# Spacing the weight decodes of a linear-attention and two-MLP kernel: one empty part more in the first group, a pace of 2.5 and three empty parts in the two whole-product MLP pairs

## The chip, the cores and the metric

The kernel runs on one core of a Trainium2 chip. The metric is the device time of one execution in microseconds (us). The engines are TensorE (PE in the profile, PEld for its weight loads), VectorE (DVE), ScalarE (ACT), GpSimd (POOL) and SyncE (SP), which issues the transfers. Each engine works through its own instructions in the order in which the program wrote them and waits on semaphores for the others.

## What is computed

Linear attention over 4 x 8 heads, then two MLPs, on 2304 tokens of 512 features, in float32. The two MLPs are the part that the change touches:

```python
def _moe_ref(x, w_gate, w_val, w_out, rms_g):      # d_ff 1536: "kind 1" in the kernel
    rms = np.sqrt(np.mean(x * x, axis=-1, keepdims=True) + 1e-06)
    xn = x / rms * rms_g
    g = xn @ w_gate
    silu = g * (1.0 / (1.0 + np.exp(-g)))
    val = xn @ w_val
    return (silu * val @ w_out).astype(np.float32)

def _moe2_ref(x, w_in, w_out):                     # d_ff 2048: "kind 2"
    h = x @ w_in
    g = h * (1.0 / (1.0 + np.exp(-h)))
    return (g @ w_out).astype(np.float32)
```

The weights arrive as 64-bit floats. The kernel reads the two 32-bit words of each number and makes of them a float32 in integer arithmetic (this is what a decode does), and it then splits every float32 operand into a high half, rounded to TensorE's format, and a low half, the rest. A product is three matmuls: high x high, high x low, low x high (`PASS`).

## The kernel before

**Data.** The tokens lie in five blocks j = 0 to 4 (512 tokens each, block 4 has 256). `xs[j]` holds the inputs of the current MLP as high and low halves, `ya[j]` the sums of its outputs. The hidden features are taken in slices f of 128.

**Groups.** After the attention part the slices run in 17 groups, u = 0 to 16. Groups 0 to 8 are GLU slices f = 3 to 11 (kind 1; slices 0 to 2 come before them, in the attention part and at the start of the loop `stream`). Groups 9 to 16 are MLP pairs (kind 2, two slices f each). Most groups multiply blocks 0 and 1 in `quad`, with seven half products instead of eight: for that, sums of the weights (`sum12`, `sum34`, `shi`, `slo`) and sums of the tokens (`token_sums`: `whole` on VectorE L345, `less` on GpSimd L319, `tok_high` on ScalarE L328, `tok_low` on VectorE L331) are made. The first two MLP pairs, u = 9 and 10 (`std <= u < std + NSTD`), take the whole products of blocks 0 and 1 instead, in `mlp_block`; the tokens' sums of the new `xs` are made beside them. These are the whole-product pairs, pair 1 and pair 2 below.

**What a block's product sets off.** In a GLU slice: matmuls for g (L205), Silu on ScalarE (L222), matmuls for v, s = s * v on VectorE (L228), and `split_h`, that is the high half of h on ScalarE (L198) and the low half on VectorE (L199). In an MLP slice: matmuls (L205), Silu (L239, or L661 in `mlp_block`), and `split_h`. Later come the output products of a block, four of them (`g2_glu`, L259, or `g2_mlp`, L292), which read both halves of h, and whose results are added to `ya` by VectorE (L270 in the GLU, L303 in the MLP; in pair 1 ScalarE copies them, L301). The outputs go through a ring of four PSUM buffers named y. In the last GLU slice L270 is followed by the halves of the next MLP's inputs (L272 on ScalarE, L249 on VectorE).

**The weight queue.** `WeightQueue` holds a list of jobs, here called parts. Each part is a count of free weight slots that it needs and some functions, and a part `(0,)` has none and is empty. The functions are:

- `dec(key, n)`: five VectorE steps on the words of a weight (L146, L149, L152, L154, L157) and two GpSimd integer adds (L160). The weight lies in the buffers raw0, m0 or raw1, m1.
- `load(u, key, n)`: a DMA of 512 KB on SP's queue into raw0 or raw1, for the next weight that uses that buffer. It stands in the same part behind the `dec` that frees the buffer.
- `hi(key)`: ScalarE writes the high half (L412); for g and v it first scales the rows (L168, four steps).
- `lo(key)`: VectorE writes the low half (L416); then the weight can be used.
- `shi`, `slo`: the same for the sums of the weights, L412 and L416.

Here a0 and a1 are the two weights that a group's first products use (g and v, or the two `i`), and bs those of its output products (o, or the two `p`).

**What sets the order.** The program writes TensorE's work by the generator `stream`. Each `yield` hands out the time of some matmuls (matmuls x columns / 2365 us). The loop at the end adds it to `due`; when `due` is over the pace it issues the next part (`tick`) and takes the pace off. The pace is `A_PACE` 1.8 up to u = 8 and `M_PACE` 2.0 after that. While `hold` is set no part goes; `need` issues parts at once until a weight is ready. In `g1_glu` and `proj` the yield comes ahead of the matmuls, and in `g2_glu` and `g2_mlp` behind them. So a part's instructions stand in each engine's order at the place where the sum passed the pace: a decode in front of L228 is done before L228. The tokens' sums come out one by one the same way, by `gone`.

In pair 1, `each` says how many output products of the last GLU slice follow each half of an `mlp_block`: the pairs of numbers are for the first and second half. The jobs of pair 1 itself are issued in groups 7 and 8; a job that needs 1 << 10 slots ends them and holds the queue until pair 1's products of blocks 0 and 1 are out. Then the jobs of pair 2 go, beside pair 1's other blocks, and the jobs of group 11 behind them.

Of the kernel before, what the change touches and what calls it, by code (L numbers as in the profile page):

```python
# [20 lines left out]
def kernel(  # L21
# [168 lines left out]

    PASS = [(0, 0), (0, 1), (1, 0)]
    HALVES = [slice(0, 64), slice(64, P)]
    M_PACE, A_PACE, T_PACE = 2.0, 1.8, 1.2
    W_EARLY, GRAIN, GATE = 3, 3, 3

    def split_h(s, j):
# [114 lines left out]
    NSTD = 2  # L311
    std = next(u for u, g in enumerate(groups) if g[0] == 2)
# [55 lines left out]
    class WeightQueue:  # L368
# [28 lines left out]
        def plan(self, u):  # L397
            kind, _ = groups[u]
            (a0, a1), bs = self.keys(u)
            st = self.st  # L400
            ss = State()
            ss.t = {}
            hw = KH * P
            mf = lambda key: st[key].m.bitcast(F32)

            def dec(key, n):
                for k in range(7):
                    w_decode((0, 0, key, None), st[key], k, n)

            def split_hi(x, tl):  # L410
                v = tl.rearrange("p (a n) -> p a n", a=2)
                nc.scalar.activation(out=v[:, 0, :], in_=x, func=AF.Copy)  # L412
                return v

            def split_lo(x, v, eng=nc.vector):
                eng.tensor_tensor(out=v[:, 1, :], in0=x, in1=v[:, 0, :].bitcast(F32), op=ALU.subtract)  # L416

            def hi(key):
                if key[1] in "gv":
                    w_scale(st[key])  # L420
                st[key].t = split_hi(mf(key), self.slot(key))

            def lo(key):
                split_lo(mf(key), st[key].t)
                wt[key] = st[key].t

            def sum12():
                ss.x = pools["w"][1].tile([P, KC * P], F32, tag="ws", name="ws", bufs=1)
                m0, m1 = mf(a0), mf(a1)
                less(ss.x[:, :hw], m1[:, :hw], m1[:, hw:], ALU.add)  # L430
                less(ss.x[:, hw:], ss.x[:, :hw], m0[:, :hw])

            def sum34():
                m0, m1 = mf(a0), mf(a1)
                less(m1[:, :hw], m0[:, :hw], m1[:, :hw])
                less(m1[:, hw:], m0[:, hw:], ss.x[:, hw:])

            def shi(n):
                ss.t[n] = split_hi(ss.x if n == 0 else mf(a1), self.slot(("s", u, n)))

            def slo(n):
                split_lo(ss.x if n == 0 else mf(a1), ss.t[n], nc.vector if kind == 2 else nc.gpsimd)
                wt["s", u, n] = ss.t[n]

            load = self.load
            if u == 0:
                jobs = [
                    (0, lambda: dec(a0, 0), lambda: load(u, bs[0], 0)),
                    (0,),
                    (0, lambda: dec(a1, 1), lambda: load(u + 1, 1, 1)),  # L450
                    (1, lambda: hi(a0)),
                    (0, lambda: lo(a0)),
                    (1, lambda: hi(a1)),
                    (0, lambda: lo(a1), sum12),
                    (0, sum34),
                    (1, lambda: shi(0)),
                    (0, lambda: slo(0), lambda: dec(bs[0], 0), lambda: load(u + 1, 0, 0)),
                    (1, lambda: shi(1)),
                    (0, lambda: slo(1)),
                ]  # L460
                self.tail = [(1, lambda: hi(bs[0])), (0, lambda: lo(bs[0]))]
            elif kind == 1:
                jobs = [
                    (0, lambda: dec(a1, 1), lambda: load(u + 1, 1, 1)),
                    *self.tail,
                    (0, lambda: dec(a0, 0), lambda: load(u, bs[0], 0)),
                    (1, lambda: hi(a1)),
                    (0, lambda: lo(a1)),
                    (1, lambda: hi(a0)),
                    (0, lambda: lo(a0), sum12),  # L470
                    (0, sum34),
                    (1, lambda: shi(0)),
                    (0, lambda: slo(0), lambda: dec(bs[0], 0), lambda: load(u + 1, 0, 0)),
                    (1, lambda: shi(1)),
                    (0, lambda: slo(1)),
                ]
                self.tail = [(1, lambda: hi(bs[0])), (0, lambda: lo(bs[0]))]
            elif std <= u < std + NSTD:
                jobs = [
                    (0, lambda: dec(a1, 1), lambda: load(u, bs[1], 1)),  # L480
                    *self.tail,
                    (0, lambda: dec(a0, 0), lambda: load(u, bs[0], 0)),
                    (1, lambda: hi(a1)),
                    (0, lambda: lo(a1)),
                    (0, lambda: dec(bs[1], 1), lambda: load(u + 1, 1, 1)),
                    (1, lambda: hi(a0)),
                    (0, lambda: lo(a0)),
                    (0, lambda: dec(bs[0], 0), lambda: load(u + 1, 0, 0)),
                    (1, lambda: hi(bs[1])),
                    (0, lambda: lo(bs[1])),  # L490
                    (0,),
                    (1, lambda: hi(bs[0])),
                    (0, lambda: lo(bs[0])),
                ]
                self.tail = []
                if u == std:
                    jobs.append((1 << 10,))
            else:
                jobs = [
                    (0, lambda: dec(a0, 0)),  # L500
                    (0, lambda: dec(a1, 1), lambda: load(u, bs[0], 0)),
                    (1, lambda: hi(a0), lambda: load(u, bs[1], 1)),
                    (1, lambda: lo(a0), lambda: hi(a1)),
                    (0, lambda: lo(a1), sum12),
                    (0, sum34),
                    (1, lambda: shi(0)),
                    (0, lambda: slo(0)),
                    (1, lambda: shi(1), lambda: dec(bs[0], 0)),
                    (0, lambda: slo(1), lambda: load(u + 1, 0, 0)),
                    (1, lambda: hi(bs[0]), lambda: dec(bs[1], 1)),  # L510
                    (0, lambda: lo(bs[0]), lambda: load(u + 1, 1, 1)),
                    (1, lambda: hi(bs[1])),
                    (0, lambda: lo(bs[1])),
                ]
            self.jobs += [(n, fns) for n, *fns in jobs]
# [13 lines left out]
    wq = WeightQueue()  # L529
# [144 lines left out]
    def stream():  # L674
# [25 lines left out]
        for u, (kind, fs) in enumerate(groups):  # L700
            first, last = kind == 2 and fs[0] == 0, u == len(groups) - 1
            done = u + 1 == std
            wq.pace = A_PACE if u < std else M_PACE
            hs = {j: {} for j in range(NB)}
            if std <= u < std + NSTD:
                out_of = lambda j: g2_mlp(fs, j, hs[j], first, False, False)
# [1 line left out]
                wq.hold = first  # L708
                while wait:
                    wait.pop(0)()  # L710
                each = [(2, 1)] * 4 if first else [(2, 2), (1, 1), (0, 0), (0, 0)]
                for n, k in enumerate(each):
                    if n == 3:
                        ys = chain_of(ys, out_of(0))
# [856 lines left out]
```

## Time and profile before

| | |
|---|---|
| median of 3 runs | 963.65 us (962.95 to 964.86) |
| the profiled execution | 964.62 us |
| its span, first to last instruction | 962.7 us |
| mean granted clock of TensorE | 0.994 |
| TensorE / weight loads | 947.6 / 793.8 us busy |
| VectorE | 709.2 us busy |
| ScalarE | 432.8 us busy |
| GpSimd | 415.3 us busy |
| DMA | 60.42 MB, mean 63 GB/s |

The rows below are from the profiled execution, in us from the start of its span. A timeline row gives the start, the time from there to the end of the last instruction of the row, the engine, the line and the operation with what it writes and reads, and how many; in brackets stands how long the engine was idle before and who released it. The end of a matmul is modelled; matmuls overlap, so their pace is read from the starts. The attention part takes the first 180 us, the GLU slices run to about 565 us, pair 1 to about 612 us, pair 2 to about 664 us, and the other six MLP pairs to the end.

### The profile page before, as it was taken

What the parts mean: (1) busy time and instruction counts of PE and PEld (TensorE: products, weight loads), DVE (VectorE), ACT (ScalarE), POOL (GpSimd) and SP (SyncE); (2) the same over time, 40 slices, a digit from 0 to 9 for tenths busy, and PEclk for the clock granted to TensorE, in tenths of its full rate; (3) what the DMA queues carried; (4) which work ended last, traced back from release to release, by engine and by line L of the source; (5) the groups of instructions that cost most, each with busy time, mean ns of one, the idle gap of its engine ahead of it and who ended that gap; (6) DMA issues with size and microseconds to landing.
All of it is one profiled execution on the core that took longest, in us unless ns stands there. A gap on an engine that the chain in (4) does not pass through costs nothing.

```text
span 962.7 us, 17025 instructions
## 1 busy us (share of the span) xinstructions
PE 947.6 (98%) x6570; PEld 793.8 (82%) x6570; DVE 709.2 (74%) x1368; ACT 432.8 (45%) x978; POOL 415.3 (43%) x402
## 2 busy tenths in 40 slices
PE   8999999998999999999999999999999999999998
PEld 6888878887888888888888886788888888888887
DVE  6998989656687778788779785886666666767653
ACT  6999877543334424333333345433333333333321
POOL 8888645315455336436335204632424242424200
PEclk9999999999999999999999999999999999999999
DMA  8655543002120121022012101111111111111023
GB/s 188 174 134 136 138 122 101 9 23 66 44 78 32 44 66 45 22 65 66 22 45 66 44 1 44 45 44 44 44 45 45 44 44 44 44 44 45 1 77 121
DMA packets 79489, 60.42 MB, mean 63 GB/s; under 512 B 27312, under 2 KB 73648, under 8 KB 79408
## 3 DMA queue, kind: packets, MB, share of 16 engines
q1 hardware_dynamic: 79136, 59.26, 21.1%
q8 instruction: 52, 0.85, 0.4%
q14 instruction: 29, 0.24, 0.1%
q10 hardware_dynamic: 272, 0.07, 0.0%
HBM read 49.87 MB, written 4.72 MB: 57 GB/s over the span
## 4 chain that ended last, share of the span: by engine, by line
PE 90%; DVE 4%; ACT 2%; DMA 1%; POOL 1%; SPq 1%; issue 1%; DVEq 0%; POOLq 0%
PE g L205 22%; PE y L292 20%; PE g L535 15%; PE y L259 13%; PE y L205 6%; PE b L1039 3%; PE b L205 2%; PE b L1439 2%; PE kv L1119 2%; PE b L1012 2%; PE b L1223 2%; PE b L1199 1%; PE b L1319 1%; POOL m L160 1%; DVE h L199 1%
## 5 line engine op out<-in xcount | busy, mean ns | idle before, releaser
L160 POOL TENSOR_TENSOR m<-m,raw 128x512 int32<-128x512 int32 x136 | 204.1, 1503 | 323.7 <-issue 176.9
L205 PE MATMUL g<-xs,w 128*128 128x512 f32 x1056 | 256.3, 389 | 0.0
L205 PEld LDWEIGHTS g<-xs,w 128*128 128x128 f32 x1056 | 197.4, 188 | 40.5
L292 PE MATMUL y<-w,h 128*128 128x512 f32 (+1 forms) x870 | 209.4, 390 | 4.2 <-DVE h L199 3.3
L292 PEld LDWEIGHTS y<-w,h 128*128 128x128 f32 x870 | 163.1, 189 | 40.0 <-DVE h L199 4.7
L259 PE MATMUL y<-h,w 128*128 128x512 f32 (+1 forms) x648 | 157.4, 369 | 2.7 <-ACT h L198 2.5
L199 DVE TENSOR_TENSOR h<-s,h 128x512 fp32r<-128x512 f32 (+1 forms) x134 | 108.4, 815 | 65.5 <-ACT h L198 64.2
L270 DVE TENSOR_TENSOR ya<-y,ya 128x512 f32<-128x512 f32 (+1 forms) x200 | 123.0, 631 | 22.5 <-PE y L259 22.4
L259 PEld LDWEIGHTS y<-h,w 128*128 128x128 f32 x648 | 114.4, 190 | 24.0 <-ACT h L198 2.9
L303 DVE TENSOR_TENSOR ya<-y,ya 128x512 f32<-128x512 f32 (+1 forms) x127 | 84.6, 680 | 60.2 <-PE y L292 59.6
L198 ACT ACTIVATE h<-s 128x512 fp32r<-128x512 f32 (+1 forms) x134 | 77.2, 586 | 100.3 <-DVE s L640 46.2
L535 PE MATMUL g<-xs,w 128*128 128x512 f32 x360 | 91.7, 390 | 0.0
L412 ACT ACTIVATE w<-m 128x512 fp32r<-128x512 f32 x74 | 46.6, 630 | 90.3 <-POOL m L160 72.7
L416 DVE TENSOR_TENSOR w<-m,w 128x512 fp32r<-128x512 f32 x65 | 65.7, 1012 | 27.5 <-ACT w L412 27.5
L1088 ACT ACTIVATE e<-b,nb 128x128 f32<-128x128 f32 x272 | 76.1, 425 | 7.7 <-PE b L205 2.8
L535 PEld LDWEIGHTS g<-xs,w 128*128 128x128 f32 x360 | 67.1, 188 | 13.9
L535 PE MATMUL g<-w,w 128*128 128x512 f32 x270 | 68.8, 390 | 0.0
L205 PEld LDWEIGHTS y<-xs,w 128*128 128x128 f32 x480 | 60.6, 188 | 2.3
L205 PE MATMUL y<-xs,w 128*128 128x256 f32 x480 | 61.3, 280 | 0.0
L535 PEld LDWEIGHTS g<-w,w 128*128 128x128 f32 x270 | 50.1, 188 | 10.0
L1056 DVE TENSOR_REDUCE small<-b 128x4 f32<-128x512 f32 (+1 forms) x80 | 51.4, 642 | 8.0 <-PE b L1039 4.5
L558 ACT ACTIVATE s<-s 128x512 f32<-128x512 f32 x21 | 13.3, 632 | 77.7 <-DVE s L563 77.7
(120 smaller groups left out, 1164.3 us busy)
## 6 DMA issues: line engine op xcount, KB each, us to landing
raw<-in_moe_w_out_dram SPq DMA_DIRECT2D x28, 512.0 KB, 3.6
raw<-in_moe_w_in_dram SPq DMA_DIRECT2D x16, 512.0 KB, 3.7
raw<-in_moe_w_gate_dram SPq DMA_DIRECT2D x12, 512.0 KB, 3.7
raw<-in_moe_w_val_dram SPq DMA_DIRECT2D x12, 512.0 KB, 3.7
qT<-e SPq DMA_DIRECT2D x72, 64.0 KB, 2.7
x<-in_k_dram SPq DMA_DIRECT2D x16, 256.0 KB, 3.7
x<-in_q_dram SPq DMA_DIRECT2D x16, 256.0 KB, 3.3
va<-in_v_dram SPq DMA_DIRECT2D x32, 128.0 KB, 4.1
```

Source lines behind the costliest of these rows:

```text
L160: tt(out=mi, in0=mi, in1=(low if step == 5 else high).bitcast(I32), op=ALU.add)
L198: nc.scalar.activation(out=ht[:, 0, :], in_=s, func=AF.Copy)
L199: nc.vector.tensor_tensor(out=ht[:, 1, :], in0=s, in1=ht[:, 0, :].bitcast(F32), op=ALU.subtract)
L205: nc.tensor.matmul(out=ps, lhsT=w[:, a, cc * P:(cc + 1) * P], rhs=xs[j][:, c, cc, :], start=(n == 0), stop=(n == 3 * KC - 1),)
L259: nc.tensor.matmul(out=ps, lhsT=wt[1, "o", f][:, a, d * P:(d + 1) * P], rhs=hs[f][:, c, :], start=(n == 0), stop=(n == nn - 1),)
L270: nc.vector.tensor_tensor(out=y[:, d, :], in0=ps, in1=y[:, d, :], op=ALU.add)
L292: nc.tensor.matmul(out=ps, lhsT=hs[f][:, a, t * P:(t + 1) * P], rhs=wt[2, "p", f][:, c, d0:d1], start=(n == 0), stop=(n == nn - 1),)
L303: nc.vector.tensor_tensor(out=o[:, t, d0:d1], in0=ps, in1=o[:, t, d0:d1], op=ALU.add)
L416: eng.tensor_tensor(out=v[:, 1, :], in0=x, in1=v[:, 0, :].bitcast(F32), op=ALU.subtract)
L535: nc.tensor.matmul(out=ps, lhsT=w[:, a, (c0 + c) * P:(c0 + c + 1) * P], rhs=x(b, c), start=(start and n == 0), stop=(n == 3 * KH - 1), ski ...
L1056: nc.vector.tensor_reduce(out=st.mx.rearrange("p (j e) -> p e j", e=2)[:, e], in_=st.ps[e], axis=AX.X, op=ALU.max)
L1088: nc.scalar.activation(out=st.e[r][:, :, h, :] if blocks4 else st.e[r][:, h, :], in_=src.rearrange("p (a f) -> p a f", a=4) if blocks4 els ...
```

## The change

Three things are changed. In group 0 a second empty part stands between the two decodes, so that `dec(a1)` and all parts behind it go one part later. In the two whole-product pairs three empty parts are added (before the second `dec`, behind it, and between the decode of the last weight and the high half of the other `p`), and from u = 9 to u = 10 the pace is a new constant, 2.5, instead of 2.0. In pair 1 the output products of the last GLU slice are spread otherwise over the four `mlp_block`s: 2 and 1, 2 and 2, 1 and 0, 2 and the rest, instead of 2 and 1 each. No arithmetic is changed, none is added and none is removed.

```diff
--- before.py
+++ after.py
@@ -190,7 +190,7 @@
 
     PASS = [(0, 0), (0, 1), (1, 0)]
     HALVES = [slice(0, 64), slice(64, P)]
-    M_PACE, A_PACE, T_PACE = 2.0, 1.8, 1.2
+    M_PACE, A_PACE, S_PACE, T_PACE = 2.0, 1.8, 2.5, 1.2
     W_EARLY, GRAIN, GATE = 3, 3, 3
 
     def split_h(s, j):
@@ -446,6 +446,7 @@
             if u == 0:
                 jobs = [
                     (0, lambda: dec(a0, 0), lambda: load(u, bs[0], 0)),
+                    (0,),
                     (0,),
                     (0, lambda: dec(a1, 1), lambda: load(u + 1, 1, 1)),
                     (1, lambda: hi(a0)),
@@ -479,13 +480,16 @@
                 jobs = [
                     (0, lambda: dec(a1, 1), lambda: load(u, bs[1], 1)),
                     *self.tail,
+                    (0,),
                     (0, lambda: dec(a0, 0), lambda: load(u, bs[0], 0)),
+                    (0,),
                     (1, lambda: hi(a1)),
                     (0, lambda: lo(a1)),
                     (0, lambda: dec(bs[1], 1), lambda: load(u + 1, 1, 1)),
                     (1, lambda: hi(a0)),
                     (0, lambda: lo(a0)),
                     (0, lambda: dec(bs[0], 0), lambda: load(u + 1, 0, 0)),
+                    (0,),
                     (1, lambda: hi(bs[1])),
                     (0, lambda: lo(bs[1])),
                     (0,),
@@ -700,7 +704,7 @@
         for u, (kind, fs) in enumerate(groups):
             first, last = kind == 2 and fs[0] == 0, u == len(groups) - 1
             done = u + 1 == std
-            wq.pace = A_PACE if u < std else M_PACE
+            wq.pace = A_PACE if u < std else S_PACE if u < std + NSTD else M_PACE
             hs = {j: {} for j in range(NB)}
             if std <= u < std + NSTD:
                 out_of = lambda j: g2_mlp(fs, j, hs[j], first, False, False)
@@ -708,7 +712,7 @@
                 wq.hold = first
                 while wait:
                     wait.pop(0)()
-                each = [(2, 1)] * 4 if first else [(2, 2), (1, 1), (0, 0), (0, 0)]
+                each = [(2, 1), (2, 2), (1, 0), (2, 1)] if first else [(2, 2), (1, 1), (0, 0), (0, 0)]
                 for n, k in enumerate(each):
                     if n == 3:
                         ys = chain_of(ys, out_of(0))
```

## Rows read from the trace of the kernel before

**Rows 1.** The page, busy us per engine (share of the span) x instructions.

```profile
PE 947.6 (98%) x6570; PEld 793.8 (82%) x6570; DVE 709.2 (74%) x1368; ACT 432.8 (45%) x978; POOL 415.3 (43%) x402
```

**Rows 2.** Waits of TensorE: engine, line, releaser; us, times, longest.

```profile
PE y L292 <- DVE h L199: 3.3, 1, 3.3
...
PE y L292 <- DVE ya L270: 0.8, 1, 0.8
```

**Rows 3.** Windows: stretch, length; busy (count) per engine; PEclk, DMA share, GB/s.

```profile
250.00:560.00 310.00, 310.00 (x1520) 262.62 (x1520) 243.57 (x439) 111.15 (x228) 137.18 (x111) 1.00 0.15 47
...
223.18:228.20 5.02, 4.79 (x13) 3.57 (x14) 3.30 (x5) 4.04 (x11) 3.12 (x4) 0.66 0.36 115
...
580.00:584.00 4.00, 3.51 (x15) 2.93 (x16) 2.52 (x8) 2.69 (x6) 0.00 (x0) 1.00 0.00 0
...
604.00:608.00 4.00, 4.00 (x13) 3.12 (x13) 4.00 (x3) 1.20 (x2) 2.32 (x2) 0.70 0.09 16
```

**Rows 4.** Timeline of TensorE, 215 to 237 us: start, us, what [idle before].

```profile
215.12 5.60 PE L205 MATMUL g<-xs,w 128*128 128x512 f32 x24
...
223.18 0.49 PE L259 MATMUL y<-h,w 128*128 128x512 f32 x1 [2.46 <-ACT h L198]
...
228.11 5.62 PE L205 MATMUL g<-xs,w 128*128 128x512 f32 x24
...
236.29 2.88 PE L205 MATMUL g<-xs,w 128*128 128x512 f32 x12
```

**Rows 5.** Timeline of VectorE around the second decode, 215 to 222 us.

```profile
215.70 0.42 DVE L146 TENSOR_SCALAR m<-raw 128x512 uint32<-128x512 uint32 x1
...
217.38 1.28 DVE L270 TENSOR_TENSOR ya<-y,ya 128x512 f32<-128x512 f32 x2
219.36 1.17 DVE L146 TENSOR_SCALAR m<-raw 128x512 uint32<-128x512 uint32 x1 [0.70 <-DMA raw<-in_moe_w_val_dram]
...
221.79 0.67 DVE L228 TENSOR_TENSOR s<-s,g 128x512 f32<-128x512 f32 x1
```

**Rows 6.** Timeline of TensorE in the first whole-product pair.

```profile
578.10 1.55 PE L292 MATMUL y<-w,h 128*128 128x512 f32 x6
580.49 4.38 PE L292 MATMUL y<-w,h 128*128 128x512 f32 x18 [0.83 <-DVE ya L270]
...
592.87 5.60 PE L205 MATMUL g<-xs,w 128*128 128x512 f32 x24
...
609.38 2.88 PE L205 MATMUL g<-xs,w 128*128 128x512 f32 x12
```

**Rows 7.** Timeline of GpSimd, ScalarE and VectorE in the same pair.

```profile
590.33 3.84 POOL L160 TENSOR_TENSOR m<-m,raw 128x512 int32<-128x512 int32 x1 [41.50 <-ACT ya L301]
...
595.58 0.63 ACT L412 ACTIVATE w<-m 128x512 fp32r<-128x512 f32 x1 [4.64 <-POOL m L160]
...
599.14 2.46 DVE L146 TENSOR_SCALAR m<-raw 128x512 uint32<-128x512 uint32 x1
```

**Rows 8.** Timeline of VectorE and GpSimd in the second pair.

```profile
622.29 1.54 DVE L146 TENSOR_SCALAR m<-raw 128x512 uint32<-128x512 uint32 x1
...
623.75 1.54 DVE L149 TENSOR_SCALAR raw<-raw 128x512 uint32<-128x512 uint32 x1
...
623.63 1.38 POOL L160 TENSOR_TENSOR m<-m,raw 128x512 int32<-128x512 int32 x1
```

**Rows 9.** Timeline of three engines in the second pair, 631 to 641 us.

```profile
631.16 1.22 DVE L345 TENSOR_TENSOR w<-xs 128x1024 f32<-128x1024 f32 x1
...
632.46 2.40 POOL L319 TENSOR_TENSOR w<-w,w 128x1024 f32<-128x1024 f32 x1 [3.05 <-DVE w L345]
...
637.19 0.63 ACT L412 ACTIVATE w<-ws 128x512 fp32r<-128x512 f32 x1 [3.92 <-POOL ws L319]
...
638.34 0.64 ACT L198 ACTIVATE h<-s 128x512 fp32r<-128x512 f32 x1
...
640.85 0.69 DVE L199 TENSOR_TENSOR h<-s,h 128x512 fp32r<-128x512 f32 x1
```

## The prediction

> **What bounds the kernel now.** I read the busy shares first: TensorE is busy for 98% of the span [rows 1]. That leaves some 15 us, and only where TensorE stands still can moving a decode gain anything. So the view of waits, for TensorE alone, comes next: one long wait for the low half h (L199) and a short one for an accumulation on VectorE (L270) [rows 2]; the third of weight stands in the timeline, 2.46 us before L259 [rows 4]. Then the windows: from 250 to 560 us TensorE is busy for 310.00 of 310.00 us [rows 3], so group 1 to 8 can give nothing. Everything lies in two places, the matmuls around group 0's decodes (220 us) and the first whole-product pair (578 to 609 us).
>
> A wait costs more than its idle time. After the two long ones the granted clock falls: 0.66 and 0.70 in the windows behind them, while it stays at 1.00 behind the short one [rows 3]; of the two levels, 1.2 and 2.4 GHz, the engine runs some matmuls at the lower. So I price a wait from start to start. Undisturbed, 36 matmuls of 512 columns take 236.29 - 228.11 = 8.18 us, 0.227 each [rows 4].
>
> - Group 0: 228.11 - 215.12 = 12.99 us for 36 matmuls; 8.18 would do. Loss 4.8 us.
> - Pair 1, late wait: 609.38 - 592.87 = 16.51 us for 48 matmuls; 10.9 would do. Loss 5.6 us.
> - Pair 1, early wait: 580.49 - 578.10 = 2.39 us for 6 matmuls; 1.36 would do. Loss 1.0 us [rows 6].
>
> **Group 0, one empty part more.** I counted the loop through by its sums: every yield adds its matmul time to `due`, a part goes when `due` is over 1.8. Before, `dec(a1)` goes at the yield ahead of block 0's value product, so its five VectorE steps stand ahead of that block's L228, which makes s and with it h. `dec(a1)` waits 0.70 us for its DMA, starts at 219.36, and its first step takes 1.17 instead of 0.42 us; L228 starts only at 221.79 [rows 5]. After, that part is empty, and `dec(a1)` goes at the next yield, behind L228, L198 and L199 of this block. L228 then starts when the two L270 are done, 217.38 + 1.28 = 218.7. It takes 0.7, L198 0.64, L199 0.69 [rows 9]: 220.7. TensorE ends the 24 matmuls before at 215.12 + 5.45 = 220.6 and needs the low half with its second matmul, at 220.8. The wait goes; if a GpSimd add holds L199, up to 0.1 stays. I take 4.7 of 4.8 us.
>
> What is late next? `dec(a1)` now runs 220.7 to 222.4 (five steps take 217.38 - 215.70 = 1.68 us [rows 5]); its two GpSimd adds follow, to 225.4; then ScalarE scales and rounds, to 227.5; only then comes L198 of block 2, and its L199 ends near 228.9. TensorE wants that at 220.6 + 36 x 0.227 = 228.8 and 229.0. So it just fits; a slip costs a few tenths, and I keep 0 to 0.4. The load that the part issues goes one part later on SP's queue, which has nothing behind it; it fell at 215.81 and landed before 219.4, so it is no longer waited for. All later jobs of groups 0 to 3 go one part later. That costs nothing as long as the weights come before their product; the cover is a TensorE that is never idle there [rows 3], and without it a part costs 1.8 us.
>
> **Pair 1, early wait.** With the four `each` entries changed, the half of h that L199 makes of block 1 is ahead of the last four accumulations in VectorE's queue instead of between them. By the same count the first product finds its buffer (four y buffers go round) at most 0.3 us late instead of 1.0. I take 0.7 (0.3 to 1.0). The jobs of pair 1 itself, with three empty parts, now reach into the last GLU group, 545 to 556 us, where VectorE also finishes xs: one low half more is due there and its operations may be held by two adds. A y buffer is wanted again four y products on, each with six to twelve other matmuls in front (four times 9 x 0.227 = 8 us), and TensorE never idles there before [rows 3], so I cost it at nothing; without this cover it is the 1.0 us of the early wait. Both halves of `p` come later too, and their first use, at 578 us, is 22 us off.
>
> **Pair 1, late wait.** Before, both i decodes are issued back to back. The first GpSimd add takes 3.84 us, ScalarE's `hi` waits for it until 595.58 (4.64 us idle), and behind `hi` in ScalarE's order stand copies, Silu and the h halves that TensorE needs next. Then a third decode stands ahead of the last L199, its first step held for 2.46 us [rows 7]. With pace 2.5 and empty parts, my count gives: first i decode, empty, second i decode, empty, `hi` behind both halves of h for block 2, and the p decode behind those of block 3. GpSimd's queue then holds the adds of both decodes, then the first token subtraction, then the p decode's adds. So ScalarE reaches Silu of the first half right behind its copies of y, which end when TensorE enters the next product (592.87 [rows 6]) and two steps of about 0.6 later, at 593.7 to 594.2; with L198 (0.64) and L199 (0.69), held by an add at most 1.3, that h is ready by 596.2. The second half's product ends 12 x 0.227 after 592.87, at 595.7; Silu, L198 and L199 bring 597.9, held 598.9. TensorE comes to y of block 2 at 592.87 + 24 x 0.227 = 598.4 and needs the last half of h five matmuls later, at 599.5. The whole 5.6 us goes, with 0.6 us in hand.
>
> **Pair 2: where work piles up.** Five parts that were over before pair 2's first y product now fall into its y products. Before, ScalarE's `shi` (637.19) stood ahead of Silu and L198 there, and L199 came at 640.85, in time [rows 9]. After, the `hi` of the next group's first i stands there, and it waits for two adds of a decode that has only just gone out. Take the start of y of block 0 as zero. TensorE needs the low half of the second f at 36 x 0.227 + 5 x 0.227 = 9.3. Up to -5.4 (24 matmuls before) all is paced by TensorE. From there, one behind the other: a copy, p's `hi`, Silu and L198 on ScalarE (four steps of about 0.6, with the 0.2 us that TensorE's last result takes) to -2.8; L199 (0.69) to -2.1; the last token sum on VectorE (1.22 [rows 9]) to -0.9; p's low half (0.7) to -0.2, needed at 0.2; GpSimd's token subtraction (2.40 [rows 9]) to 1.7, which holds VectorE's next L199 to 2.4; the decode of the next group's first i (1.68) to 4.0; its first add (1.38 [rows 8]) to 5.4. Meanwhile VectorE does two y sums and begins the next decode. If operations of the two alternate, as in rows 8 (first step 1.54 us, an add in between, second step 1.54 us), add two ends at 7.1, `hi` at 7.7, Silu and L198 at 8.9, but VectorE still has the rest of its decode and two y sums: L199 at 10.5. Wait: 1.2 us. If the decode runs on while GpSimd stands, as beside the 3.84 us add [rows 7], `hi` is 1.2 later and the wait 2.3. Bounds: 0 (all held operations fall well) to 2.3 plus the clock. I take 1.2, since rows 8 are the same operations in the same stretch, and rows 7 an add after 41 us of rest. A loss of 1.0 us left the clock at 1.00 [rows 3, 6], so none is added.
>
> The Trainium skill (SBUF — State Buffer, Who interferes with whom) says that VectorE and GpSimd share a port pair, held by whichever starts first for its whole instruction. By it an add could wait for one VectorE instruction only and the sum would be the one with 1.2; rows 8 agree, the 3.84 us of rows 7, over seven VectorE operations, doesn't.
>
> **Sum.** 964.62 (profiled execution) - 4.7 - 0.7 - 5.6 + 1.2 = 954.8; it lay 1.0 us above the median of the runs, so 953.9 against 963.65.
>
> **Rivals.**
> - No new wait in pair 2: 963.65 - 11.0 = 952.6. For it: each held operation is counted at its worst somewhere. Against: ScalarE's order is fixed.
> - The new wait is long: 2.3 us, and the clock falls as behind the two long ones. There 4.8 us of loss stood beside 2.46 us of waiting [rows 4], and 5.6 beside 3.3 [rows 2]: 2.3 us more in both. 952.6 + 2.3 + 2.3 = 957.2. For it: rows 7 show such an add. Against: rows 8.
> - The late wait of pair 1 stays in part: GpSimd's token subtraction (2.40) gets ahead of L199, 1.7 us of wait (to 601.2 instead of 599.5) and 2.3 for the clock: 953.9 + 4.0 = 957.9. For it: only 0.6 us is in hand. Against: L199 waits since 597.2 and GpSimd's subtraction comes after an add that lasts to 598.2.
> - Slower: ScalarE stands behind GpSimd not once but in the four blocks that follow (`hi`, `hi`, `shi`, `shi` each ahead of a Silu). At the price of the long wait, 4.6 each: 952.6 + 18.4 = 971.0. It is slower from 13 / 4 = 3.3 us for each. Against it: the second `hi` is ready some 6 us before its block's product.
> - The parts don't land where I count them, because a product calls for its weights and draws the jobs forward: 963.65. Against it: by my count no product comes before its weights, in either kernel.
>
> **How the numbers follow.** Forecast 0.52 (952.9 to 955.2), no new wait 0.15, long wait 0.15, part of the late wait 0.09, slower 0.04, nothing moved 0.05. 0.2% is 1.9 us, about what a measurement can tell from no change. The first four are faster: 0.91. Same 0.05, slower 0.04. The range runs from 952.0 (nothing new, all of the early wait) to 958.3 (957.9 and the few tenths of group 0).
>
> **What would show it.** Right: no wait of L259 near 220 us and a clock of 1.00 there; L146 no longer between L270 and L228; in pair 1 no wait of L292 for L199; the decodes further apart; one wait of about 1.2 us for L199 near 632 us with ScalarE's L412 behind GpSimd's L160. Wrong, if TensorE waits in pair 1 still, or in group 0 some 8 us later for the next block's h, or if the 545 to 578 us stretch shows idle time on TensorE.

## The result, and the profile after

| | before | after |
|---|---|---|
| median, us | 964.21 (962.95 to 964.86, 4 runs) | 954.24 (953.92 to 954.74, 4 runs) |
| ratio, 95% interval | | 0.9899 (0.9881 to 0.9916) |
| profiled execution, its span, us | 964.62, 962.7 | 954.74, 952.9 |
| mean granted clock | 0.994 | 1.000 |

The kernel became 1.0% faster. The two long waits are gone; one short wait grew and one is new.

The page of the kernel after, busy us of the engines [rows 1]:

```profile
PE 942.4 (99%) x6570; PEld 791.5 (83%) x6570; DVE 705.6 (74%) x1368; ACT 431.9 (45%) x978; POOL 414.0 (43%) x402
```

TensorE's instructions are the same 6570, and its busy time fell by 5.2 us: most of that is the matmuls of group 0 and pair 1 that no longer run at the lower clock. The waits of TensorE in the kernel after, us, times, longest [rows 2]:

```profile
PE y L292 <- DVE ya L270: 1.6, 1, 1.6
...
PE y L292 <- DVE h L199: 0.7, 1, 0.7
```

The names are those of [rows 2], but the wait of 3.3 us for L199 was in pair 1 and is gone, and the 0.7 us are new and in pair 2. The 1.6 us for L270 stand where the 0.8 us stood. The windows of the kernel after [rows 3]:

```profile
250.00:560.00 310.00, 310.00 (x1515) 262.44 (x1514) 244.59 (x442) 112.38 (x231) 135.84 (x111) 1.00 0.15 46
218.00:224.00 6.00, 6.00 (x27) 4.75 (x26) 5.30 (x11) 3.03 (x7) 3.54 (x4) 1.00 0.29 92
574.00:580.00 6.00, 5.55 (x24) 4.61 (x25) 2.82 (x8) 3.27 (x7) 0.00 (x0) 1.00 0.00 0
```

TensorE never stands still from 250 to 560 us, as before, although all jobs of groups 0 to 3 go one part later. In group 0 the clock is 1.00 where it was 0.66, and it is 1.00 behind the wait of 1.6 us too. The timeline of TensorE in the kernel after, group 0, pair 1 and pair 2 [rows 4, 6]:

```profile
214.38 5.60 PE L205 MATMUL g<-xs,w 128*128 128x512 f32 x24
...
222.73 5.60 PE L205 MATMUL g<-xs,w 128*128 128x512 f32 x24
...
571.97 0.87 PE L259 MATMUL y<-h,w 128*128 128x256 f32 x6
574.45 5.73 PE L292 MATMUL y<-w,h 128*128 128x512 f32 x24 [1.61 <-DVE ya L270]
...
588.17 5.60 PE L205 MATMUL g<-xs,w 128*128 128x512 f32 x24
...
599.05 2.88 PE L205 MATMUL g<-xs,w 128*128 128x512 f32 x12
...
631.84 1.30 PE L292 MATMUL y<-w,h 128*128 128x512 f32 x5
633.83 4.60 PE L292 MATMUL y<-w,h 128*128 128x512 f32 x19 [0.69 <-DVE h L199]
638.27 5.60 PE L205 MATMUL g<-xs,w 128*128 128x512 f32 x24
```

From start to start, as the prediction priced it (24 matmuls take 5.44 us):

| place | before | after | difference |
|---|---|---|---|
| group 0, 36 matmuls | 12.99 | 222.73 - 214.38 = 8.35 | -4.64 |
| pair 1, y of block 0, lost | 584.71 - 578.10 - 5.44 = 1.17 | 580.01 - 571.97 - 0.71 (six matmuls of 256 columns) - 5.44 = 1.89 | +0.72 |
| pair 1, late, 48 matmuls | 16.51 | 599.05 - 588.17 = 10.88 | -5.63 |
| pair 2, y of block 1, lost | 0 | 638.27 - 631.84 - 5.44 = 0.99 | +0.99 |
| pair 2, y of block 2, lost | 658.83 - 653.04 - 5.44 = 0.35 | 0 | -0.35 |
| attention part, up to the first row | 215.12 | 214.38 | -0.74 |

That sums to -9.65 of the 9.8 us between the spans. The last line of the table is not the change's: that part is the same in both kernels. From 128 to 140 us, in that part, the granted clock was 0.86 in the execution before and 1.00 in the one after.

### The profile page after: what moved, and what is told of

The parts are those of the page before. It is cut to its first block, busy times and chain, and to the rows that moved or that the text cites. A ratio compares the mean times of both kernels' runs of the same rounds, so it can differ in the third digit from the quotient of the medians.

```text
span 952.9 us, 17029 instructions
## 1 busy us (share of the span) xinstructions
PE 942.4 (99%) x6570; PEld 791.5 (83%) x6570; DVE 705.6 (74%) x1368; ACT 431.9 (45%) x978; POOL 414.0 (43%) x402
## 4 chain that ended last, share of the span: by engine, by line
PE 93%; DVE 3%; ACT 1%; DMA 1%; POOL 1%; SPq 1%; issue 0%; DVEq 0%
PE g L205 23%; PE y L292 20%; PE g L539 15%; PE y L259 13%; PE y L205 6%; PE b L1043 3%; PE b L205 2%; PE b L1443 2%; PE kv L1123 2%; PE b L1227 2%; PE b L1016 2%; PE b L1203 1%; PE b L1323 1%; DVE h L199 1%; SPq L1183 0%
## 5 line engine op out<-in xcount | busy, mean ns | idle before, releaser
L160 POOL TENSOR_TENSOR m<-m,raw 128x512 int32<-128x512 int32 x136 | 202.5, 1491 | 322.3 <-issue 209.2
L292 PE MATMUL y<-w,h 128*128 128x512 f32 (+1 forms) x870 | 206.9, 388 | 2.3 <-DVE ya L270 1.6
L292 PEld LDWEIGHTS y<-w,h 128*128 128x128 f32 x870 | 162.4, 188 | 36.4 <-issue 1.8
L199 DVE TENSOR_TENSOR h<-s,h 128x512 fp32r<-128x512 f32 (+1 forms) x134 | 107.8, 809 | 77.5 <-ACT h L198 76.4
L259 PE MATMUL y<-h,w 128*128 128x512 f32 (+1 forms) x648 | 155.4, 366 | 0.0
L270 DVE TENSOR_TENSOR ya<-y,ya 128x512 f32<-128x512 f32 (+1 forms) x200 | 122.8, 631 | 20.9 <-PE y L259 20.7
L259 PEld LDWEIGHTS y<-h,w 128*128 128x128 f32 x648 | 113.2, 188 | 20.4 <-DVE h L199 0.5
L198 ACT ACTIVATE h<-s 128x512 fp32r<-128x512 f32 (+1 forms) x134 | 77.1, 585 | 93.7 <-DVE s L644 49.4
L412 ACT ACTIVATE w<-m 128x512 fp32r<-128x512 f32 x74 | 46.6, 629 | 84.0 <-POOL m L160 77.4
L416 DVE TENSOR_TENSOR w<-m,w 128x512 fp32r<-128x512 f32 x65 | 66.5, 1024 | 22.2 <-ACT w L412 21.1
```

The costliest lines, as they stand in the source:

```text
L160: tt(out=mi, in0=mi, in1=(low if step == 5 else high).bitcast(I32), op=ALU.add)
L198: nc.scalar.activation(out=ht[:, 0, :], in_=s, func=AF.Copy)
L199: nc.vector.tensor_tensor(out=ht[:, 1, :], in0=s, in1=ht[:, 0, :].bitcast(F32), op=ALU.subtract)
L259: nc.tensor.matmul(out=ps, lhsT=wt[1, "o", f][:, a, d * P:(d + 1) * P], rhs=hs[f][:, c, :], start=(n == 0), stop=(n == nn - 1),)
L270: nc.vector.tensor_tensor(out=y[:, d, :], in0=ps, in1=y[:, d, :], op=ALU.add)
L292: nc.tensor.matmul(out=ps, lhsT=hs[f][:, a, t * P:(t + 1) * P], rhs=wt[2, "p", f][:, c, d0:d1], start=(n == 0), stop=(n == nn - 1),)
```

## The experiments

The first four ran beside the kernel before at 964.48 us, the next four beside it at 963.47, the last two beside it at 964.38; each ratio is to the kernel before on the same chip. Every run computes all of the function.

**Group 0 alone.** The kernel before with the second empty part in group 0.

```diff
+                    (0,),
                     (0, lambda: dec(a1, 1), lambda: load(u + 1, 1, 1)),
```

> The kernel before with only the second empty part of group 0. Theory (three separate places, prices add up): the wait of L259 for L198 near 220 us is gone and with it the lower clock behind it, 4.6 to 4.8 us less than before, near 959.5; the waits of the first whole-product pair stay as they were (0.8 and 3.3 us). Rival (the decode only passes its delay on to the next block): a wait of L259 some 8 us later, at most 1 to 2 us gained, 962 or more.

959.51 us (958.88 to 961.42), ratio 0.9955 (0.9938 to 0.9971). The timeline of TensorE in this kernel:

```profile
214.62 5.60 PE L205 MATMUL g<-xs,w 128*128 128x512 f32 x24
...
222.98 5.60 PE L205 MATMUL g<-xs,w 128*128 128x512 f32 x24
```

8.36 us for the 36 matmuls, and the waits of pair 1 stand as before (3.3 and 0.8). The group 0 part is worth what it was priced at.

**The pairs alone.** The kernel after without that empty part.

```diff
-                    (0,),
                     (0, lambda: dec(a1, 1), lambda: load(u + 1, 1, 1)),
```

> The changed kernel with group 0 as before. Theory: 4.6 us more than the changed kernel, near 958.9, with the 2.46 us wait back near 220 us and no long wait of L292 for L199 in the first pair. Rival (the shifted queue of group 0 is needed for the pairs too, since all parts behind it come later): the first pair still waits, 960.5 or more.

959.19 us (957.45 to 959.38), ratio 0.9944 (0.9928 to 0.996). Group 0's wait is back, unchanged, in this kernel's timeline:

```profile
222.57 4.78 PE L259 MATMUL y<-h,w 128*128 128x512 f32 x12 [2.46 <-ACT h L198]
```

The two parts add up: (964.48 - 959.51) + (964.48 - 959.19) = 10.26, and after lies 9.97 below before. An effect of one on the other can't be told.

**The output products as before.** The kernel after with the old `each`; this asks who made the 1.6 us wait.

```diff
-                each = [(2, 1), (2, 2), (1, 0), (2, 1)] if first else [(2, 2), (1, 1), (0, 0), (0, 0)]
+                each = [(2, 1)] * 4 if first else [(2, 2), (1, 1), (0, 0), (0, 0)]
```

> The changed kernel with the old spread of output products, 2 and 1 after each block. Theory (the new spread made the early wait of the first pair longer, 1.8 instead of 1.0 us, because both last low halves of h and one more low half of xs now stand ahead of all four accumulations of block 4): 0.7 us less, near 953.5, with the L270 wait back at 0.8. Rival (the spread pays elsewhere, in the long wait that is gone): the long wait is back in part, 955 or more.

954.25 us (953.54 to 955.72), ratio 0.9899 (0.9885 to 0.9914). Its timeline:

```profile
574.01 1.55 PE L292 MATMUL y<-w,h 128*128 128x512 f32 x6
576.39 4.37 PE L292 MATMUL y<-w,h 128*128 128x512 f32 x18 [0.83 <-DVE ya L270]
```

The next product starts at 580.60, so this block loses 580.60 - 574.01 - 5.44 = 1.15 us, as before the change, against 1.89. So the new `each` made that wait longer. In the medians these 0.7 us don't show (954.25 against 954.24), and 953.5 was expected: the trace shows who made the wait, the time doesn't show what it cost.

**The output products in front.** If the buffer is freed late because the last accumulations stand behind too much, then more products in the first blocks should free it in time.

```diff
-                each = [(2, 1), (2, 2), (1, 0), (2, 1)] if first else [(2, 2), (1, 1), (0, 0), (0, 0)]
+                each = [(2, 2), (2, 2), (2, 1), (1, 1)] if first else [(2, 2), (1, 1), (0, 0), (0, 0)]
```

> The changed kernel with the output products earlier: 2 and 2, 2 and 2, 2 and 1, 1 and the rest. Theory (the early wait is VectorE's order: accumulations of block 4 behind a low half of h that waits for ScalarE): three of the four accumulations stand ahead of it, the buffers are free in time, no wait of L292 for L270 remains: 1.7 us less than the changed kernel, near 952.5. Rival (VectorE is simply full there, 1.3 us of work for each product against 1.36 of matmuls): it falls behind in block 3 and TensorE waits there for a buffer, 954 or more.

952.49 us (952.32 to 952.89), ratio 0.9878 (0.9862 to 0.9894). The timeline of TensorE and VectorE in this kernel:

```profile
572.69 5.60 PE L292 MATMUL y<-w,h 128*128 128x512 f32 x24
...
571.72 0.75 DVE L270 TENSOR_TENSOR ya<-y,ya 128x256 f32<-128x256 f32 x2
```

The two accumulations of block 4 that free the buffers start 1.0 us ahead of the product, and the product waits for nothing. They stand behind the L199 of one `mlp_block` earlier than in the kernel after. So the early wait comes from where L270 stands in VectorE's order, and the rival falls: TensorE waits for no buffer.

**The old pace.** The kernel after with 2.0 instead of 2.5, the empty parts kept.

```diff
-    M_PACE, A_PACE, S_PACE, T_PACE = 2.0, 1.8, 2.5, 1.2
+    M_PACE, A_PACE, S_PACE, T_PACE = 2.0, 1.8, 2.0, 1.2
```

> The changed kernel with its pace of 2.5 put back to 2.0; the empty parts stay. Theory (the empty parts alone keep the high half of the first i and the p decode behind the h that TensorE needs): no long wait in the first pair; in the second pair the next group's decodes go some three parts earlier, ahead of the y products, so that the 0.7 us wait goes as well: 953.4. Rival (the pace does the work): the wait of L292 for L199 in the first pair is back with 2 us or more and the lower clock, 957 or more.

957.82 us (956.78 to 958.12), ratio 0.9939 (0.9924 to 0.9953). TensorE's timeline:

```profile
594.04 5.66 PE L292 MATMUL y<-w,h 128*128 128x512 f32 x24
...
608.58 1.88 PE L292 MATMUL y<-w,h 128*128 128x512 f32 x7 [0.81 <-DVE h L199]
...
634.33 0.93 PE L292 MATMUL y<-w,h 128*128 128x512 f32 x3 [0.74 <-DVE ya L303]
636.03 5.35 PE L292 MATMUL y<-w,h 128*128 128x512 f32 x21 [0.77 <-ACT h L198]
```

A miss for the theory, and the time of the rival without its cause. Pair 1's long wait is away with the empty parts alone, but without the pace three short waits come: at 608.58 the block takes 610.30 - 606.47 - 2.72 = 1.11 us too long, y of block 1 in pair 2 takes 641.22 - 633.42 - 5.44 = 2.36, and block 2 keeps its 0.35. That is 3.8 us against 0.99 in after. Beside the empty parts the pace is worth some 3.6 us in the medians, about as much as the empty parts beside the pace (958.02 without them), and its worth lies in pair 2 and the end of pair 1, where the kernel before had no such wait.

**The pace alone.** The kernel after without the three empty parts.

```diff
                     *self.tail,
-                    (0,),
                     (0, lambda: dec(a0, 0), lambda: load(u, bs[0], 0)),
-                    (0,),
                     (1, lambda: hi(a1)),
...
                     (0, lambda: dec(bs[0], 0), lambda: load(u + 1, 0, 0)),
-                    (0,),
```

> The changed kernel without its three empty parts in the pairs; the pace of 2.5 stays. The high half of the first i then stands ahead of Silu of block 2 on ScalarE again, as in the kernel before, but the p decode stays behind the last low half of h on VectorE. Theory (the long wait was VectorE's: the third decode, held by GpSimd, ahead of the last L199): only 0.5 to 1 us of waiting in the first pair, 954 to 955. Rival (it was ScalarE's: the high half that waits for GpSimd's adds, ahead of Silu): the long wait stays, 3 us and the clock, 958 to 960.

958.02 us (957.46 to 959.14), ratio 0.9944 (0.9929 to 0.9959). The timeline of TensorE, GpSimd, ScalarE and VectorE:

```profile
592.86 1.49 PE L292 MATMUL y<-w,h 128*128 128x512 f32 x5
596.74 7.49 PE L292 MATMUL y<-w,h 128*128 128x512 f32 x19 [2.40 <-DVE h L199]
...
592.72 2.82 POOL L319 TENSOR_TENSOR w<-w,w 128x1024 f32<-128x1024 f32 x1
...
592.92 0.63 ACT L198 ACTIVATE h<-s 128x512 fp32r<-128x512 f32 x1
...
592.44 0.87 DVE L199 TENSOR_TENSOR h<-s,h 128x512 fp32r<-128x512 f32 x1 [4.88 <-ACT h L198]
593.23 2.85 DVE L416 TENSOR_TENSOR w<-m,w 128x512 fp32r<-128x512 f32 x1
596.01 0.68 DVE L199 TENSOR_TENSOR h<-s,h 128x512 fp32r<-128x512 f32 x1
```

The late wait is back: 2.40 us of it. The time is the rival's (ScalarE's `hi` ahead of Silu). The rows show which step came last: the high half for this L199 is there at 592.92 + 0.63 = 593.55, so L199 could have ended at 594.24, and TensorE wanted it at 592.86 + 5 x 0.227 = 594.0. In that step ScalarE is late by 0.2 us. The rest is the low half of a weight (L416) that stands ahead of L199 on VectorE and is held by the token subtraction on GpSimd. This does not put the rival out: before the L199 at 592.44 VectorE had stood idle for 4.88 us, waiting for a high half of h that stands behind the `hi` on ScalarE, and that `hi` (590.13) had waited 3.28 us for GpSimd. The late `hi` can have brought L416 beside the subtraction. The last two runs take the subtraction off GpSimd.

**Two empty parts less in pair 2,** on the kernel with the products in front, so that pair 2's decodes come earlier.

```diff
-                    (0,),
+                    *([(0,)] if u == std else []),
                     (1, lambda: hi(bs[1])),
                     (0, lambda: lo(bs[1])),
-                    (0,),
+                    *([(0,)] if u == std else []),
```

> The kernel with the products earlier (x4_each_front), and in the second pair only the first two of the four empty parts, so that the next group's decodes go two parts earlier there. Theory (the 0.7 us wait in the second pair is the next group's decodes and high half ahead of h): it goes, 0.9 us less than 952.5, near 951.6. Rival (the decodes then meet the token sums and the p halves, and the wait only moves): 952.3 or more, with a wait of L292 for another L199 or L416.

952.13 us (951.47 to 953.44), ratio 0.9883 (0.9866 to 0.99): no difference to 952.49 that can be told, and the wait is 0.62 instead of 0.69 us. The timeline of GpSimd and VectorE in this kernel:

```profile
627.29 2.40 POOL L319 TENSOR_TENSOR w<-w,w 128x1024 f32<-128x1024 f32 x1
...
628.03 2.21 DVE L416 TENSOR_TENSOR w<-m,w 128x512 fp32r<-128x512 f32 x1 [0.33 <-ACT w L412]
```

A miss, and what the rival said: the decodes moved, but the token subtraction now holds the L416 in front of the same L199 (630.17). The wait only changed its cause.

**The last token subtraction on VectorE,** on the same kernel. If GpSimd's subtraction is what pushes pair 2's work late, taking it off GpSimd should end the wait (`eng` is nc.vector, handed over in pair 1's call of `token_sums`).

```diff
-            lambda: less(u[3], u[3], u[2]),
+            lambda: eng.tensor_tensor(out=u[3], in0=u[3], in1=u[2], op=ALU.subtract),
```

> x4_each_front with the last token subtraction of the second pair (2.77 us on GpSimd) on VectorE instead, some 1.2 us there. Theory (GpSimd's subtraction holds VectorE's L199, 2.88 instead of 0.69 us, and so delays the decode and the h behind it): VectorE gains 2.2 and pays 1.2, the last L199 comes 1 us earlier and the 0.7 us wait goes, near 951.6. Rival (no hold; VectorE's own work is what delays it): VectorE has 1.2 us more to do, the wait grows to 1.9, near 953.7.

951.87 us (951.7 to 952.32), ratio 0.988 (0.9865 to 0.9894). The timeline of TensorE and VectorE:

```profile
629.78 5.62 PE L292 MATMUL y<-w,h 128*128 128x512 f32 x24
...
621.63 1.22 DVE L359 TENSOR_TENSOR w<-w,w 128x1024 f32<-128x1024 f32 x1
```

The subtraction takes 1.22 us of VectorE instead of 2.77 of GpSimd plus 2.2 of a held VectorE, and y of block 1 has no wait, so the rival (a wait of 1.9 us) falls. This is the lowest of all medians, and of TensorE's waits none is left for L259 or L292. The time alone can tell it neither from the run above nor from the kernel that it changes (ratios 0.988 and 0.9878); the trace does.

**The first token subtraction on VectorE,** once in the kernel with the pace alone, once in the kernel before.

```diff
-            lambda: less(u[0], u[1], u[0]),
+            lambda: nc.vector.tensor_tensor(out=u[0], in0=u[1], in1=u[0], op=ALU.subtract),
```

> The kernel with the new pace, without the three empty parts, and with the first token subtraction of pair 1 made by VectorE (1.2 us) instead of GpSimd (2.8 us). Theory, the held low half: in the run without the empty parts VectorE's low half L416 stood in front of the L199 that TensorE waited for and was held from 593.23 to 596.08 by that subtraction, while this L199's high half was there at 593.55. Without the subtraction on GpSimd L416 takes 0.7, L199 ends near 594.5, TensorE wants it at 594.0: a wait of at most 0.4 us, clock 1.00, some 5 us less than 958.0: 953.0. Rival, ScalarE's order: the high half at 590.13, behind GpSimd's adds, makes the Silus late, and a subtraction changes nothing: a wait of 2.4 us and 958.0 again.

955.74 us (955.15 to 956.99), ratio 0.9913 (0.9898 to 0.9928). The timeline of TensorE and VectorE:

```profile
595.77 4.60 PE L292 MATMUL y<-w,h 128*128 128x512 f32 x19 [1.36 <-DVE h L199]
...
593.30 1.21 DVE L351 TENSOR_TENSOR w<-w,w 128x1024 f32<-128x1024 f32 x1
594.44 0.68 DVE L416 TENSOR_TENSOR w<-m,w 128x512 fp32r<-128x512 f32 x1
```

L416 is no longer held (0.68 instead of 2.85) and the block loses 600.21 - 592.92 - 5.44 = 1.85 us instead of 604.07 - 592.86 - 5.44 = 5.77. ScalarE's work is where it was, so the rival as it was put, 2.4 us and 958.0 again, falls, and the hold of L416 is shown. Less was won than expected, since the subtraction itself (1.21) came to stand ahead of L199. VectorE again stood idle for 4.88 us, for ScalarE, before the L199 in front of it; what a `hi` in time would have saved stays open.

> The kernel before with the first token subtraction of pair 1 made by VectorE instead of GpSimd, nothing else. Theory, the held step: of the 3.3 us wait the 2.46 us of the third decode's first step are GpSimd's subtraction (598.50 to 601.32); without it the decode takes 1.7 us, ends at 600.8 and L199 near 601.5 (before: 603.6), so a wait of 1.2 us stays, which leaves the clock up: 963.5 - 2.1 - 2.3 = 959.1. Rival, the long first add: ScalarE is late by the 3.84 us add of 590.33, its last h comes at 599.5 whatever GpSimd does then, and other adds hold L199 in the subtraction's place: 963.5.

962.39 us (961.09 to 964.37, 10 runs), ratio 0.9979 (0.9968 to 0.999). The timeline of TensorE and VectorE in this kernel:

```profile
601.80 6.22 PE L292 MATMUL y<-w,h 128*128 128x512 f32 x19 [2.27 <-DVE h L199]
...
598.26 1.21 DVE L351 TENSOR_TENSOR w<-w,w 128x1024 f32<-128x1024 f32 x1
599.39 0.41 DVE L146 TENSOR_SCALAR m<-raw 128x512 uint32<-128x512 uint32 x1
```

The decode's first step takes 0.41 instead of 2.46 us [rows 7], but the subtraction stands ahead of it, so the wait falls by 1.05 only, from 3.32 to 2.27, and the clock still falls. The block took 607.87 - 597.65 = 10.22 us, before 10.98. A miss: less than half of the expected 4.4 us came (0.76 in the trace; 2.0 in the medians, 1.0 to 3.1 by the interval), and the time is nearer to the rival's 963.5 than to 959.1. The high half is ready at 598.11 + 0.63 = 598.74, TensorE wants the low half at 598.8: in the last step ScalarE is again late by 0.6, and L351 and the decode, 1.21 + 1.68, make the rest. Both come so late because VectorE had stood idle before them for ScalarE, 3.24 us ahead of the L416 at 595.50 for the `hi` behind the long add, and 1.01 us ahead of the L199 at 597.63. So the rival's cause, the long first add, is not ruled out.

## Why the prediction was right, and where it was wrong

**Group 0: right, -4.64 for -4.7.** VectorE's timeline in the kernel after shows the order that was counted [rows 5]:

```profile
217.84 0.68 DVE L228 TENSOR_TENSOR s<-s,g 128x512 f32<-128x512 f32 x1
219.22 0.83 DVE L199 TENSOR_TENSOR h<-s,h 128x512 fp32r<-128x512 f32 x1 [0.70 <-ACT h L198]
219.97 0.41 DVE L146 TENSOR_SCALAR m<-raw 128x512 uint32<-128x512 uint32 x1
```

The decode is behind L199. L228 starts at 217.84 where it was 221.79, and the decode's L146 takes 0.41 instead of 1.17 us. Of the 0.17 us that stay (8.35 for 8.18) the "up to 0.1" of a held L199 makes 0.14 (0.83 instead of 0.69). The next block's h comes in time: its L259 starts at 228.17, 5.44 behind 222.73.

**Pair 1, late: right, -5.63 for -5.6; how the loss divides between the two causes stays open.** The prediction told two causes, ScalarE behind GpSimd's long add, and a held decode ahead of the last L199. ScalarE's and VectorE's timelines in the kernel before:

```profile
598.86 0.63 ACT L198 ACTIVATE h<-s 128x512 fp32r<-128x512 f32 x1
...
596.25 1.12 DVE L416 TENSOR_TENSOR w<-m,w 128x512 fp32r<-128x512 f32 x1 [3.24 <-ACT w L412]
```

The high half was ready at 598.86 + 0.63 = 599.49 and the low half could have come at 600.2; TensorE wanted it at 599.5. In this last step ScalarE was 0.7 us late, and VectorE's queue made 3.4 of the 4.1 us to 603.60; the three runs with pace or subtraction changed give 0.2, 0.3 and 0.6 for ScalarE. But VectorE's queue was itself late by ScalarE: its L416 waited 3.24 us for the `hi` that stood behind the long add [rows 7], and the decode comes after it. No run takes away the long add alone, so the shares are not shown. The change removes both. TensorE's stretch lies 4.70 us earlier than before (588.17 for 592.87); less these, the two low halves were predicted for 591.5 and 593.2, and they ended at 591.41 and 593.13. The long add itself came again, and TensorE did not wait for it:

```profile
585.64 3.84 POOL L160 TENSOR_TENSOR m<-m,raw 128x512 int32<-128x512 int32 x1 [41.82 <-issue]
...
587.90 0.42 DVE L157 TENSOR_SCALAR m<-m 128x512 uint32<-128x512 uint32 x1
```

(the timeline of GpSimd and VectorE in the kernel after). The count that put `hi` behind both halves of h for block 2 held: L412 is at 592.26, behind L198 at 591.72.

**Pair 1, early: wrong, +0.72 for -0.7.** The step that failed is "by the same count the first product finds its buffer at most 0.3 us late". VectorE's timeline in the kernel after:

```profile
572.67 0.69 DVE L199 TENSOR_TENSOR h<-s,h 128x512 fp32r<-128x512 f32 x1 [1.25 <-ACT h L198]
573.28 0.68 DVE L249 TENSOR_TENSOR xs<-ya,xs 128x512 fp32r<-128x512 f32 x1
573.88 0.75 DVE L270 TENSOR_TENSOR ya<-y,ya 128x256 f32<-128x256 f32 x2
```

L199 is ahead of the last four accumulations, as said. But it waits there for its high half: VectorE stands idle for 1.25 us and everything behind stands with it. ScalarE brings that half only at 572.64 because an L272 (570.86) and a Silu come first. And behind L199 the low half of block 3's inputs (L249) comes ahead of the first L270 that frees a buffer. The prediction speaks of neither. The buffer is free at 574.3, the product was due at 571.97 + 0.71 = 572.68. Moving L199 forward does not bring it earlier, it brings the others later. The run with the products in front shows the same lines in an order that costs nothing. Two of the prediction's own signs of being wrong are there: TensorE still waits in pair 1, and it stands idle in the stretch from 545 to 578 us.

**Pair 2: right, 0.99 for 1.2; with block 2's old 0.35 gone, net 0.64.** The timeline of GpSimd, VectorE and ScalarE in the kernel after [rows 8, 9]:

```profile
622.65 2.77 POOL L319 TENSOR_TENSOR w<-w,w 128x1024 f32<-128x1024 f32 x1 [8.01 <-DVE w L345]
623.09 2.88 DVE L199 TENSOR_TENSOR h<-s,h 128x512 fp32r<-128x512 f32 x1
...
627.78 2.76 POOL L160 TENSOR_TENSOR m<-m,raw 128x512 int32<-128x512 int32 x2 [2.36 <-issue]
629.30 1.53 DVE L149 TENSOR_SCALAR raw<-raw 128x512 uint32<-128x512 uint32 x1
630.57 0.63 ACT L412 ACTIVATE w<-m 128x512 fp32r<-128x512 f32 x1 [8.15 <-POOL m L160]
...
632.96 0.82 DVE L199 TENSOR_TENSOR h<-s,h 128x512 fp32r<-128x512 f32 x1
```

Ends of the chain, from the start of y of block 0 (623.68):

| step | predicted | measured |
|---|---|---|
| token subtraction (L319) | 1.7 | 1.74 |
| held L199 | 2.4 | 2.29 |
| decode, with L157 | 4.0 | 3.97 |
| two adds (L160) | 7.1 | 6.86 |
| `hi` (L412) | 7.7 | 7.52 |
| Silu, L198 | 8.9 | 8.68 |
| L199; needed at 9.3 | 10.5 | 10.10 |

Each step is within 0.4 us of where it was put. What is less is the hold: the second decode lost 1.1 us on one step (1.53 instead of 0.42), not on two. The choice of [rows 8] over [rows 7] for the price of an add decided this term, and that it came out right is partly luck: its reason, that the add of [rows 7] came after 41 us of rest, does not hold. With the old pace an add in pair 2 (620.72) came after 7.02 us of rest and took 4.35 us. The clock stayed up, as said.

The Trainium skill (SBUF — State Buffer, Who interferes with whom) says that of a VectorE instruction that contends (one with two SBUF inputs does) and a GpSimd one, whoever issues first holds the shared port pair for its whole instruction while the other blocks fully. The held L199 agrees: it starts 0.44 us after the subtraction and ends 0.55 after it. The add at 585.64 doesn't: it lasted over six VectorE instructions, not one, and so did the one of [rows 7] (six, where the prediction counts seven).

**The rivals.** The late wait that stays in part (957.9) did not occur, but the run with the pace alone shows its mechanism, GpSimd's token subtraction held against the work ahead of L199. Its 958.02 us come near the price by luck: pair 1 lost 5.77 us where 4.0 were priced, and pair 2 had no wait of L292 where 1.2 stood in the sum. The long wait's price, 2.3 us of waiting plus 2.3 for the clock, fits too: 2.27 us of waiting lost 10.22 - 5.44 = 4.78 us in the last run. No new wait, a slower kernel and no change did not occur.

**The sum.** 953.9 against 954.24. It holds with one sign wrong: the early wait came out 1.4 us higher than its term, and 0.6 of that came back in pair 2. What is left of the miss, 0.9 us, does not show in the profiled execution (954.8 for 954.74), because the attention part lay 0.74 lower there, which is not the change's doing. That the sum and the profiled time come within 0.1 us of each other is luck.

## What to carry to other kernels

Before a step is moved ahead on an in-order engine, ask when its own input is ready: L199 moved forward waited for ScalarE with the whole queue behind it, and the gain became a loss of the same size. Price a held step by the neighbour that holds it, and look for the longest instruction of that neighbour (here a 2.8 us token subtraction): moving that one away ended the wait in pair 2, where moving the waiting ones only exchanged the holder. Two remedies given together can have separate worth: the empty parts removed pair 1's long wait and, at the old pace, brought short waits behind it (3.5 us lost), of which 0.99 us are left at the new pace.

## What the runs showed of the hardware

**A GpSimd add that begins within a run of VectorE steps can last as long as the run.** In all twelve traces the first add of pair 1 takes 3.84 or 3.85 us, beside six VectorE operations that are not held, and it ends 1.16 to 1.17 us after the last of them: after, 589.48 and 588.32 (587.90 + 0.42); before, 594.17 and 593.01; with the pace alone, 588.72 and 587.56. Others did the same after less rest: with the old pace the add at 620.72 ended at 625.06, VectorE's run at 623.90. It is not a rule. The add in front of the one of [rows 8] began at 621.37, 0.22 us into a VectorE operation (L331), as the add at 585.64 did (L345), and there VectorE's next step waited (1.54 us) and the two alternated. What decides between the two was not tried.

**Which waits cost the clock.** Idle time ahead of L292, what the block lost from start to start, and the granted clock in a window behind it, in the profiled execution of each:

| kernel, place | idle | lost | clock behind (window) |
|---|---|---|---|
| pace alone and subtraction, pair 1 | 1.36 | 1.85 | 1.00 (597 to 604) |
| after, pair 1 early | 1.61 | 1.89 | 1.00 (574 to 580) |
| before and subtraction, pair 1 | 2.27 | 4.78 | 0.66 (602 to 607) |
| pace alone, pair 1 | 2.40 | 5.77 | 0.58 (597 to 604) |

The window behind the 2.27 us wait in the kernel before with the subtraction on VectorE:

```profile
602.00:607.00 5.00, 5.00 (x16) 3.92 (x16) 4.97 (x6) 1.66 (x3) 4.60 (x2) 0.66 0.00 2
```

16 matmuls stand in 5 us there, where 22 would at 0.227 each: the engine ran part of them at 1.2 GHz. Between the second and the third line 0.7 us of wait stand beside 2.9 us of loss, between the first and the second 0.3 us beside nothing that shows. No bound between them can be read from this: in the attention part of the kernel before the clock fell behind an idle time of 1.81 us. Nor does one kernel pay each time: over the four runs with the pace alone the mean granted clock was 0.996, 0.998, 0.998 and 1.000, at 959.14, 957.82, 957.46 and 958.22 us.
